# Linear attention and a Hyena gate on one core: two stretches of a hand-written order re-ordered, six output buffers, the last output tile in two halves

## The chip, the cores and the metric

The kernel runs on one core of a Trainium2 chip. The metric is the device time of one execution in microseconds (us). The engines are TensorE (PE, with its weight loads as PEld), VectorE (DVE), ScalarE (ACT), GpSimd (POOL) and SyncE (SP), which here only issues DMAs.

## The reference

Eight batches, eight heads, 576 positions, 64 features per head. First a linear attention per batch b and head h, then a gate with a long convolution over the 576 positions of each batch:

```python
def phi(x):                                   # w_phi: 64 x 128
    proj = x @ w_phi
    proj = proj - max(abs(proj), axis=-1)
    return concat([exp(proj), exp(-proj)])    # 256 features
q_p, k_p = phi(q), phi(k)
kv  = einsum('bhsf,bhsd->bhfd', k_p, v);  z = sum(k_p, over s)
x   = einsum('bhsf,bhfd->bhsd', q_p, kv) / (einsum('bhsf,bhf->bhs', q_p, z) + 1e-6)
x   = x, heads side by side                   # 8 x 576 x 512
x1, x2, x3 = split(x @ w_proj)                # w_proj: 512 x 1536
conv = irfft(rfft(x2, over 576) * rfft(filter_fft, over 576))
out  = (x1 * conv * x3) @ w_out               # 8 x 576 x 512, float32
```

## The kernel before

The whole program is one string, `PLAN`, of some 1540 words. A word is a method's name, its arguments and, after `@`, the first PSUM bank (0 to 7) of its result. `run` walks through the words under a manual schedule: each engine gets its instructions in the order of the words, and so does each DMA queue (SP issues stores and transposes, POOL the loads, ACT some stores at the end). There are no loops over batches: the words of up to three batches are interleaved, so that PE projects keys of one batch while it finishes another. The dependencies between engines become semaphores by themselves. So the order of the words is the one thing that says what stands ahead of what on an engine, and the bank number says which earlier reader a matmul has to wait for.

The words that the text speaks of, with batch b, head pair v, chunk c or m:

- `load,k|q|v,b`: POOL issues the load of one batch of k, q or v (L595). `trh,k|q,b,X`: SP issues the transpose of half a batch, kn to kT or qn to qT (L607).
- `Pk` (L635), `Qn` (L642), `Pq` (L669, L675): projections by w_phi on PE. `maxk`, `maxq` (L715): DVE takes the maxima from PSUM. `ex` (L697): ACT's exponentials. `mhi`, `mlo` (L739), `trm` and `trme`: the maxima, split in two bf16 parts (mh), are transposed on PE and copied to mT.
- `vs` (L757): POOL multiplies v by the keys' factor. `KV` (L772), `NE` (L786): PE's sums. `rc` (L800), `xn` (L805): DVE divides. `trx` (L824): SP issues the transpose of a quarter of xn to xT. `ptx` and `ptxe` do the same for one quarter by PE and a copy.
- `f1` (L853) and `f2` (L859): sums and differences of xn (SD, then xf), on POOL or DVE, ahead of the Fourier matmuls `Ft` (L868) and `Fs` (L875). `Fe` copies their result to XF, on ACT (L297) or DVE (L299). `X2` (L894), `Y1` (L904) and `m3` (L908): the projection in the frequency domain, the product with the filter and a sum.
- `X1`, `X3` (L916): projections x1 and x3 on PE, 8 matmuls of 256 columns each. `X1e` copies x1 to x1s. `tm` (L957) multiplies x1 by x3. `I` (L969), `Ie` (L987), `Ip`, `Im` (L990): the inverse transform. `ym` (L1004): the gate's product yT.
- `O` (L1015): one output tile of 128 positions by 512 columns, four matmuls of 512 columns. `Oe` copies it from PSUM to an `o` buffer, on ACT or DVE (L297, L299). `st` (L1024) stores 64 rows of it. Tile c = 4 holds the last positions of a pair of batches.

The buffers are rings: `RING` gives a name's count, and `turn_of` hands the next buffer of the ring to whoever asks first. A buffer is written again when its last reader has ended; for `o` that is a store that has landed.

Of the kernel before, what the change touches and what calls it, by code (L numbers as in the profile page):

```python
# [24 lines left out]
RING = {'Ekp': 4, 'Ekm': 4, 'Eqp': 3, 'Eqm': 3, 'vp': 3, 'vm': 3, 'r': 4, 'o': 4, 'kn': 2, 'qn': 2,  # L25
# [93 lines left out]
maxq,5,2@0 Pq,4,1@2 ex,q,m,4,0@4 trh,k,6,0 ex,q,p,4,0@4 ex,q,m,4,1@2 O,2,0@7 Oe,DVE,2,0@7
ex,q,p,4,1@2 X2,3,3@6 Y1,3,3@6 st,SP,2,0,1 KV,4,0@4 Pk,5,0@0 Pq,4,3@6 maxk,5,0@0 O,2,3@2  # L120
KVe,ACT,4,0@4 trxt,3 trh,q,5,0 ex,q,m,4,3@6 m3,POOL,3,1 NE,4,0@4 rc,4,0@4 ex,q,p,4,3@6 X3,3,2@3
st,SP,2,1,0 m3,POOL,3,0 xn,4,0@4 KV,4,1@6 Oe,DVE,2,3@2 load,q,6 ex,k,m,5,0@0 tm,3,2@3 ex,k,p,5,0@0
Pq,4,2@4 NE,4,1@0 rc,4,1@0 KVe,ACT,4,1@6 xn,4,1@0 f1,POOL,4,0,1 ex,q,p,4,2@4 NE,4,3@6 X2,3,4@3
rc,4,3@6 xn,4,3@6 ex,q,m,4,2@4 Y1,3,4@3 X1t,3@0 X1te,ACT,3@0 f1,POOL,4,0,0 NE,4,2@4 X3t,3@6 I,3,1@0
rc,4,2@4 f2,POOL,4,0,0 Pk,5,1@2 Ie,3,1@0 xn,4,2@4 tmt,3@6 trx,4,0 Pkt,5@6 Ip,3,1@0 Pqt,4@4 Im,3,1@0
maxkt,5@6 exqt,p,4@4 X3,3,1@0 exqt,m,4@4 f1,POOL,4,1,0 tm,3,1@0 st,SP,2,1,1 X1,3,3@1 exkt,p,5@6
exkt,m,5@6 maxk,5,1@2 I,3,0@4 Ie,3,0@4 ym,POOL,3,1 X1e,ACT,3,3@1 I,3,2@6 Ie,3,2@6 NEt,4@0 Im,3,0@4
Ip,3,0@4 ex,k,m,5,1@2 Im,3,2@6 rct,4@0 Ip,3,2@6 X3,3,3@5 ym,POOL,3,0 ex,k,p,5,1@2 xnt,4,1@0
f1,POOL,4,1,1 I,3,3@6 Ie,3,3@6 trx,4,3 em,m,5,0 trx,4,1 st,SP,2,2,0 xnt,4,0@0 tm,3,3@5 Pk,5,3@2
em,p,5,0 Qn,5,1@0 Ip,3,3@6 Qnt,5@4 trx,4,2 Im,3,3@6 maxq,5,1@0 X1,4,1@6 X3,4,1@7 maxqt,5@4  # L130
ex,k,m,5,3@2 trh,q,6,0 st,SP,2,3,0 ex,k,p,5,3@2 X1e,ACT,4,1@6 Pk,5,2@0 ex,k,p,5,2@0 f2,POOL,4,0,1
tm,4,1@7 ym,POOL,3,3 ex,k,m,5,2@0 Qn,5,0@4 maxq,5,0@4 maxk,5,2@0 ym,POOL,3,2 X1,4,0@6 vs,POOL,m,5,0
O,3,0@7 Oe,DVE,3,0@7 X1,4,2@4 mhi,5 trh,k,6,1 maxk,5,3@2 f2,POOL,4,1,1 X1e,ACT,4,0@6 X1,4,3@5
Ft,4,0,0@6 X1e,ACT,4,3@5 mlo,POOL,5 f2,POOL,4,1,0 Fs,4,1@0 X1e,ACT,4,2@4 trh,q,6,1 Fs,4,0@6 X3,4,2@5
Fe,ACT,4,1@0 yt,ACT,3 em,p,5,1 Fe,ACT,4,0@6 st,SP,3,0,1 trm,5@4 Ft,4,1,0@2 Fs,4,2@2 Fs,4,3@0
tm,4,2@5 Fe,DVE,4,3@0 st,SP,2,2,1 trme,ACT,5@4 Fe,ACT,4,2@2 Pq,5,1@6 Pq,5,0@4 Pk,6,0@2 maxk,6,0@2
O,3,2@0 Oe,DVE,3,2@0 st,SP,2,3,1 X2,4,1@1 ex,q,p,5,1@6 ex,q,m,5,1@6 trh,k,7,1 st,SP,2,0,0
vs,POOL,p,5,1 X2,4,2@6 vs,POOL,p,5,0 Y1,4,1@1 X2,4,3@7 ex,q,m,5,0@4 em,m,5,1 vs,POOL,m,5,1
ex,q,p,5,0@4 Xl,ACT,4 Y1,4,2@6 KV,5,0@4 KVe,DVE,5,0@4 Pqt,5@0 exqt,m,5@0 X2,4,0@6 Y1,4,3@7 NE,5,0@4
rc,5,0@4 xn,5,0@4 load,q,7 exqt,p,5@0 load,v,6 KV,5,1@0 Y1,4,0@6 ex,k,m,6,0@2 Pq,5,3@4 ex,k,p,6,0@2  # L140
KVe,ACT,5,1@0 ex,q,m,5,3@4 NE,5,1@2 rc,5,1@2 st,SP,3,2,1 xn,5,1@2 X2,4,4@0 Pk,6,2@6 ex,q,p,5,3@4
Y1,4,4@0 st,SP,3,0,0 m3,POOL,4,1 Pq,5,2@2 ex,q,m,5,2@2 ex,q,p,5,2@2 maxk,6,2@6 NE,5,3@4 rc,5,3@4
O,3,1@0 Oe,ACT,3,1@0 O,3,3@1 NE,5,2@2 m3,POOL,4,0 xn,5,3@4 O,3,4@0 Oe,DVE,3,3@1 ex,k,p,6,2@6
ex,k,m,6,2@6 rc,5,2@2 xn,5,2@2 NEt,5@4 rct,5@4 xnt,5,1@4 xnt,5,0@4 I,4,3@2 f1,POOL,5,0,1 X3,4,0@1
Ie,4,3@2 Ip,4,3@2 f1,DVE,5,1,1 f1,POOL,5,0,0 trxt,4 f2,DVE,5,0,0 tm,4,0@1 Oe,ACT,3,4@0 X1t,4@0
I,4,1@4 X1te,ACT,4@0 f1,DVE,5,1,0 Ie,4,1@4 Im,4,3@2 Ft,5,0,0@6 trx,5,3 st,SP,3,3,1 Ip,4,1@4
f2,POOL,5,0,1 X3t,4@2 Fs,5,1@0 trx,5,0 Fe,ACT,5,1@0 tmt,4@2 load,v,7 Fs,5,0@6 Im,4,1@4 f2,POOL,5,1,1
f2,POOL,5,1,0 X3,4,3@3 Fe,ACT,5,0@6 Ft,5,1,0@4 tm,4,3@3 Pk,6,1@6 trx,5,1 Fs,5,3@0 ym,POOL,4,1
# [52 lines left out]
class Kernel:  # L201
# [819 lines left out]
    def st(self, eng, b, c, i):  # L1021
        o = self.turn_of("o", (b, c))
# [58 lines left out]
```

## Time and profile before

| what | value |
|---|---|
| time of three runs | 299.99, 297.97, 295.18 us (median 297.97) |
| the profiled execution | 295.91 us, its span 294.0 us |
| busy | PE 272.7, DVE 248.8, ACT 223.5, POOL 229.4 us |
| mean granted clock of TensorE | 0.996 |
| DMA | 40.07 MB, mean 136 GB/s |

The profile shows one execution. "L916" is line 916 of the kernel; "a<-b" names a tile written and a tile read; "PEld" is the weight load, which overlaps with matmuls; "SPq" is SP's DMA queue, where the length of a row is how long SP needed to issue. A bracket at a row's end tells how long the engine was idle before it and what ended that.

### The profile page before, as it was taken

How to read it: one execution, taken by the hardware profiler on the slowest of the kernel's cores; microseconds unless marked ns; L12 is line 12 of the kernel's file. 1: busy time of each engine (PE TensorE's matmuls, PEld its weight loads, DVE VectorE, ACT ScalarE, POOL GpSimd, SP SyncE). 2: the span in 40 equal slices, each digit the busy share in tenths (PEclk: the TensorE clock that was granted, in tenths of full speed). 3: DMA queues.
4: the chain of work that ended last, by engine and by line, in shares of the span. 5: the costliest groups of instructions: out<-in, count | busy, mean ns of one | idle time of the engine just before them, and what ended most of it. 6: DMA issues, size and time to landing. Idle time of an engine off the chain costs nothing.

```text
span 294.0 us, 10233 instructions
## 1 busy us (share of the span) xinstructions
PE 272.7 (93%) x4297; PEld 194.9 (66%) x4332; DVE 248.8 (85%) x433; ACT 223.5 (76%) x371; POOL 229.4 (78%) x187
## 2 busy tenths in 40 slices
PE   5688999998999999999999999999999999999992
PEld 1346677666667856877478876776777666976750
DVE  6997899999989887999788978888999957687771
ACT  4999999987957787986897978968558999632421
POOL 8398894999867899999997899866948779855130
PEclk9999999999999999999999999999999999999998
DMA  7999999999899999999969945999282531222266
GB/s 138 240 207 163 164 197 168 123 203 181 131 157 199 151 162 195 161 107 187 172 112 138 211 95 108 161 138 180 61 98 50 90 75 28 21 45 56 61 130 188
DMA packets 72191, 40.07 MB, mean 136 GB/s; under 512 B 52496, under 2 KB 66960, under 8 KB 72144
## 3 DMA queue, kind: packets, MB, share of 16 engines
q1 hardware_dynamic: 56928, 22.49, 47.7%
q0 software_dynamic: 14816, 16.25, 36.7%
q8 instruction: 34, 0.56, 0.8%
q10 hardware_dynamic: 400, 0.66, 0.8%
q14 instruction: 13, 0.11, 0.1%
HBM read 33.75 MB, written 9.44 MB: 147 GB/s over the span
## 4 chain that ended last, share of the span: by engine, by line
PE 63%; DVE 5%; DMA 4%; issue 2%; ACT 2%; POOL 1%; SPq 0%; DVEq 0%; ACTq 0%; POOLq 0%
PE ps L916 15%; PE ps L894 10%; PE ps L1015 8%; PE ps L969 7%; PE ps L772 5%; PE ps L786 4%; PE ps L875 2%; PE ps L925 2%; PE ps L669 2%; PE ps L635 2%; DMA qT<-qn 2%; PE ps L675 2%; DVE mq L715 2%; PE ps L642 2%; DMA xT<-xn 1%
## 5 line engine op out<-in xcount | busy, mean ns | idle before, releaser
L916 PE MATMUL ps<-xT,wproj 128*128 128x256 bf16 x512 | 64.1, 273 | 0.5 <-DMA xT<-xn 0.4
L916 PEld LDWEIGHTS <-wproj 128*128 128x128 bf16 x512 | 48.1, 98 | 9.5 <-issue 0.6
L1004 POOL TENSOR_TENSOR yT<-cv,x1s 128x576 bf16<-128x576 f32 x31 | 39.3, 1278 | 18.5 <-DVE cv L990 16.9
L715 DVE TENSOR_REDUCE mq<-ps 128x8 f32<-128x1024 f32 (+1 forms) x40 | 43.7, 1110 | 4.1 <-PE ps L642 3.6
L715 DVE TENSOR_REDUCE mk<-ps 128x8 f32<-128x1024 f32 (+1 forms) x40 | 43.9, 1111 | 3.8 <-PE ps L635 2.6
L757 POOL TENSOR_TENSOR vm<-vn,vm 128x1152 bf16<-128x1152 bf16 x16 | 34.3, 2152 | 5.9 <-ACT vm L751 5.9
L757 POOL TENSOR_TENSOR vp<-vn,vp 128x1152 bf16<-128x1152 bf16 x16 | 34.4, 2155 | 5.6 <-ACT vp L751 5.5
L853 POOL TENSOR_TENSOR SD<-xn 128x512 bf16<-128x512 bf16 x28 | 32.0, 1153 | 7.0 <-DVE xn L805 5.4
L697 ACT ACTIVATE Eqp<-ps 128x1024 bf16<-128x1024 f32 x32 | 33.1, 1039 | 4.6 <-PE ps L675 4.5
L859 POOL TENSOR_TENSOR xf<-SD 128x512 bf16<-128x512 bf16 x27 | 30.8, 1155 | 6.7 <-DVE SD L853 6.2
L1015 PE MATMUL ps<-wout,yT 128*128 128x512 bf16 x127 | 34.8, 379 | 1.1
L697 ACT ACTIVATE Ekp<-ps 128x1024 bf16<-128x1024 f32 x32 | 33.1, 1034 | 1.9 <-PE ps L635 1.4
L697 ACT ACTIVATE Ekm<-ps 128x1024 bf16<-128x1024 f32 x32 | 33.1, 1033 | 1.3 <-DVE mk L715 0.9
L697 ACT ACTIVATE Eqm<-ps 128x1024 bf16<-128x1024 f32 x32 | 32.8, 1040 | 1.5 <-PE ps L675 1.1
L990 DVE TENSOR_TENSOR cv<-es,ps 128x288 f32<-128x288 f32 x64 | 26.4, 443 | 6.5 <-POOL yT L1004 3.7
L908 POOL TENSOR_TENSOR T<-T,T 128x1024 bf16<-128x1024 bf16 x14 | 29.6, 2127 | 2.7 <-DVE T L904 1.9
L894 PE MATMUL ps<-wproj,XF 128*128 128x512 bf16 x116 | 30.0, 379 | 1.2 <-ACT x1s L297 0.4
L969 PE MATMUL ps<-inv,T 128*128 128x288 bf16 x192 | 28.1, 286 | 0.7 <-DVE mq L715 0.4
L297 ACT COPY o<-ps 128x512 f32<-128x512 f32 x23 | 13.5, 596 | 15.9 <-PE ps L1015 13.7
L957 DVE TENSOR_TENSOR x1s<-ps,x1s 128x512 bf16<-128x512 f32 x32 | 21.8, 684 | 3.5 <-PE ps L916 2.2
L297 ACT CAST XF<-ps 128x576 bf16<-128x576 f32 x28 | 16.9, 647 | 9.2 <-PE ps L875 9.2
L297 ACT CAST x1s<-ps 128x512 bf16<-128x512 f32 (+1 forms) x32 | 16.9, 538 | 8.6 <-PE ps L916 4.2
(183 smaller groups left out, 638.2 us busy)
## 6 DMA issues: line engine op xcount, KB each, us to landing
out_dram<-o SPq DMA_DIRECT2D x67, 128.0 KB, 2.5
vn<-in_v_dram POOLq DMA_DIRECT2D x8, 576.0 KB, 8.4
kn<-in_k_dram POOLq DMA_DIRECT2D x7, 576.0 KB, 8.9
qn<-in_q_dram POOLq DMA_DIRECT2D x7, 576.0 KB, 7.9
wproj<-in_moe_w_proj_dram POOLq DMA_DIRECT2D x3, 512.0 KB, 7.8
fl<-in_moe_filter_fft_dram SPq DMA_DIRECT2D x8, 128.0 KB, 6.2
out_dram<-o ACTq DMA_DIRECT2D x5, 128.0 KB, 2.8
qn<-in_q_dram POOLq DMA_DIRECT2D x2, 288.0 KB, 7.1
```

The lines of the kernel that those rows point to most:

```text
L297: self.nc.scalar.copy(dst, src)
L697: self.nc.scalar.activation(e, p, AF.Exp, bias=0.0, scale=1.0 if g == "p" else -1.0)
L715: self.nc.vector.tensor_reduce(out=out, in_=src, axis=AX.X, op=ALU.max, apply_absolute_value=True)
L757: self.eng(eng).tensor_tensor(out=t[:, :, :, 0:64], in0=self.at("vn", b)[:, 2 * X:2 * X + 2], in1=t[:, :, :, 64:65].to_broadcast([128, 2, ...
L853: self.eng(eng).tensor_tensor(out=o[:, :, 2 * i:2 * i + 2, :], in0=x[:, :, 0:2, :], in1=x[:, :, 2:4, :], op=ALU.subtract if i else ALU.add)
L859: self.eng(eng).tensor_tensor(out=o[:, :, 2 * i:2 * i + 2, :], in0=x[:, :, 0:4:2, :], in1=x[:, :, 1:4:2, :], op=ALU.subtract if i else ALU ...
L894: self.mm(self.pb(0), l, w[:, kt, 512:1024], start=(kt == 0), stop=(kt == 3))
L908: self.eng(eng).tensor_tensor(out=Y, in0=Y, in1=self.at(f"T{2 * e + 1}", b), op=ALU.add)
L916: self.mm(o[:, d], w[:, kt, f0 + 128 * m:f0 + 128 * m + 128], y[:, 1, ::-1, ::-1] if d else y[:, 0], start=(kt == 0), stop=(kt == 3))
L969: self.mm(self.pb(e, 0, 288), l, inv[:, 2 * e + i if i < 2 else 4 + e, :], start=(i == 0), stop=(i == 2))
L1004: self.eng(eng).tensor_tensor(out=self.at("yT", b)[:, m, 0:SEQ], in0=self.turn_of("cv", (b, m)).rearrange("p x h t -> p (x h t)"), in1=sel ...
L1015: self.mm(self.pb(0), y[:, kt, 128 * c:128 * c + 128], w[:, kt, :], start=(kt == 0), stop=(kt == 3))
```

## The change

1. The stretch of the plan that runs at about 80 to 150 us (batches 1 to 3, called A below) is written in a new order with other PSUM banks. The stretch behind it keeps its order and gets other banks; the one word in it that moves is `load,v,5`, which stood ahead of the gate's products of batch 2 and now stands behind `f1,POOL,4,1,0`.
2. The stretch at about 195 to 262 us (batches 4 to 7, called B) is written in a new order, with other banks, and some words move up to the end.
3. In both, some words change engine. In A one output copy and one XF copy go from ACT to DVE. In B two output copies and two XF copies go from ACT to DVE, `f2,6,1,0` from POOL to DVE, one x1s copy and `trme,6` from DVE to ACT, `mlo,6` from DVE to POOL.
4. The ring `o` has six buffers for four.
5. The last output tile is computed, copied and stored in two halves of 256 columns (new words `Oh`, `Oeh`, `sth`), both stores on SP; before, one copy and two stores of 64 rows, on SP and ACT.

A cut of the diff: the ring, the piece of B around `X1,6,0`, the end of the plan, the new functions.

```diff
-RING = {'Ekp': 4, ... 'r': 4, 'o': 4, 'kn': 2, 'qn': 2,
+RING = {'Ekp': 4, ... 'r': 4, 'o': 6, 'kn': 2, 'qn': 2,
...
-mlo,POOL,7 f1,POOL,6,1,0 trx,6,2 O,5,3@5 f2,POOL,6,0,1 exkt,p,7@0 ptx,6,3@4 ptxe,DVE,6,3@4
-f2,POOL,6,1,0 f2,POOL,6,1,1 Oe,ACT,5,3@5 O,5,1@6 exkt,m,7@0 Oe,DVE,5,1@6 O,5,0@4 maxk,7,2@2 X1,6,0@7
-Pk,7,1@0 Oe,ACT,5,0@4 maxk,7,1@0 Ft,6,0,5@2 em,m,7,1 Fs,6,1@5 trm,7@4 em,p,7,1 X1e,ACT,6,0@7
-Fs,6,0@2 Fe,ACT,6,1@5 Fe,ACT,6,0@2 trme,DVE,7@4 em,p,7,0 ex,k,m,7,1@0 X1,6,1@7 Ft,6,1,4@2 Fs,6,2@2
...
+ex,k,p,7,2@4 f1,POOL,6,1,0 Oe,DVE,5,3@1 f1,POOL,6,1,1 exkt,p,7@2 f2,POOL,6,1,1 O,5,1@1 exkt,m,7@2
+trx,6,2 trme,DVE,7@6 Oe,ACT,5,0@7 Pk,7,1@2 maxk,7,2@4 Ft,6,0,6@4 Fs,6,0@4 Fs,6,1@6 em,m,7,1
+Oe,DVE,5,1@1 ptxe,DVE,6,3@0 ex,k,m,7,1@2 Fe,ACT,6,0@4 X1,6,0@1 maxk,7,1@2 Fe,ACT,6,1@6 X1,6,1@0
+f2,DVE,6,1,0 X1e,ACT,6,0@1 Ft,6,1,6@4 Fs,6,2@4 Fs,6,3@6 Fe,DVE,6,2@4 ex,k,p,7,1@2 X1,6,2@1
...
-st,SP,7,3,0 O,7,1@7 yt,DVE,7 Oe,ACT,7,1@7 st,SP,7,0,1 O,7,2@6 st,ACT,7,1,1 Oe,DVE,7,2@6 st,ACT,7,2,0
-st,SP,7,1,0 O,7,4@7 st,SP,7,2,1 st,ACT,7,0,0 Oe,DVE,7,4@7 st,SP,7,4,1 st,ACT,7,4,0
+yt,DVE,7 Oe,ACT,7,1@3 st,SP,7,0,1 O,7,2@2 st,ACT,7,1,1 Oe,DVE,7,2@2 st,ACT,7,2,0 st,SP,7,1,0
+Oh,7,4,0@5 Oh,7,4,1@7 st,SP,7,2,1 st,ACT,7,0,0 Oeh,DVE,7,4,0@5 sth,SP,7,4,0 Oeh,DVE,7,4,1@7
+sth,SP,7,4,1
...
+    def Oh(self, b, c, h):
+        y, w, x = self.at("yT", b - (c == 4)), self.at("wout"), slice(256 * h, 256 * h + 256)
+        for kt in range(4):
+            self.mm(self.pb(0, 0, 256), y[:, kt, 128 * c:128 * c + 128], w[:, kt, x],
+                    start=(kt == 0), stop=(kt == 3))
+    def Oeh(self, eng, b, c, h):
+        self.copy(eng, self.turn_of("o", (b, c))[:, 256 * h:256 * h + 256], self.pb(0, 0, 256))
+    def sth(self, eng, b, c, h):
+        o, x = self.turn_of("o", (b, c)), slice(256 * h, 256 * h + 256)
+        dict(SP=self.nc.sync, ACT=self.nc.scalar)[eng].dma_start(
+            out=self.out.rearrange("b (t j) d -> (b t) j d", j=9)[64 * b - 64:64 * b + 64, 4, x],
+            in_=o[:, x])
```

The functions behind `Oeh` move down by 15 lines and those ahead of them by one, so a line of the page stands one or 16 lower in the changed kernel.

How the order moves on SP in stretch A, near 125 to 142 us of the profile before. kT1 and qT1 are the transposed keys and queries of batch 5, xT1 that of batch 3, o0 to o5 the output buffers. Before:

```order
L824 DMA_TRANSPOSE xT1_134<-xn0_130 128x4x128 x4
L607 DMA_TRANSPOSE kT1_85<-kn1_79 128x9x128
L1024 DMA out_0_dram<-o0_1174 64x512
L1024 DMA out_0_dram<-o1_1175 64x512
L607 DMA_TRANSPOSE kT1_85<-kn1_79 128x9x128
L1024 DMA out_0_dram<-o0_1174 64x512
L1024 DMA out_0_dram<-o3_1177 64x512
L607 DMA_TRANSPOSE qT1_83<-qn1_77 128x9x128
L1024 DMA out_0_dram<-o2_1176 64x512
L607 DMA_TRANSPOSE kT0_84<-kn0_78 128x9x128
```

And now, on the same queue:

```order
L608 DMA_TRANSPOSE kT1_85<-kn1_79 128x9x128
L1040 DMA out_0_dram<-o4_1178 64x512
L825 DMA_TRANSPOSE xT1_134<-xn0_130 128x4x128 x4
L608 DMA_TRANSPOSE kT1_85<-kn1_79 128x9x128
L608 DMA_TRANSPOSE qT1_83<-qn1_77 128x9x128
L1040 DMA out_0_dram<-o5_1179 64x512
L1040 DMA out_0_dram<-o2_1176 64x512
L1040 DMA out_0_dram<-o1_1175 64x512
L1040 DMA out_0_dram<-o0_1174 64x512 x2
L1040 DMA out_0_dram<-o5_1179 64x512
L608 DMA_TRANSPOSE kT0_84<-kn0_78 128x9x128
```

The first kT1 goes ahead of the four xT1 transposes, and qT1 follows the second kT1 with no store between; six stores stand behind it.

On DVE in stretch B, near 226 to 243 us of the profile before, from the maxima of batch 7's keys (mk1) to the first product of Y1 (T20). Before:

```order
L715 TENSOR_REDUCE mk1_87<-ps_61 128x2x4
L715 TENSOR_REDUCE mk1_87<-ps_61 128x2x2
L299 COPY xT0_133<-ps_61 128x512
L299 COPY o0_1174<-ps_61 128x512
L715 TENSOR_REDUCE mk1_87<-ps_61 128x2x4 x2
L299 COPY mT1_93<-ps_61 128x128
L299 CAST x1s0_141<-ps_61 128x2x8x32 x2
L904 TENSOR_TENSOR T20_1165<-ps_61,HTo0_71 128x1024
```

And now:

```order
L716 TENSOR_REDUCE mk1_87<-ps_61 128x2x4
L716 TENSOR_REDUCE mk1_87<-ps_61 128x2x2
L300 COPY o5_1179<-ps_61 128x512
L300 COPY mT1_93<-ps_61 128x128
L716 TENSOR_REDUCE mk1_87<-ps_61 128x2x4
L300 COPY o1_1175<-ps_61 128x512
L300 COPY xT0_133<-ps_61 128x512
L716 TENSOR_REDUCE mk1_87<-ps_61 128x2x4
L860 TENSOR_TENSOR xf0_138<-SD0_137 128x2x256
L300 CAST XF0_139<-ps_61 128x576 x2
L300 CAST x1s0_141<-ps_61 128x2x8x32 x2
L905 TENSOR_TENSOR T20_1165<-ps_61,HTo0_71 128x1024
```

One more output copy, an f2 (xf0) and two XF copies stand ahead of the x1s copies, and the two maxima are parted by an output copy and the xT copy.

On DVE at the end, from the last gate product. Before:

```order
L957 TENSOR_TENSOR x1s0_141<-ps_61,x1s0_141 128x2x8x32
L1004 TENSOR_TENSOR yT1_1173<-cv1_1171,x1s0_141 128x576
L299 COPY o3_1177<-ps_61 128x512
L299 COPY yT0_1172<-yT1_1173 128x4x64
L299 COPY o2_1176<-ps_61 128x512
L299 COPY o3_1177<-ps_61 128x512
```

And now:

```order
L958 TENSOR_TENSOR x1s0_141<-ps_61,x1s0_141 128x2x8x32
L1005 TENSOR_TENSOR yT1_1173<-cv1_1171,x1s0_141 128x576
L300 COPY o1_1175<-ps_61 128x512
L300 COPY yT0_1172<-yT1_1173 128x4x64
L300 COPY o4_1178<-ps_61 128x512
L300 COPY o5_1179<-ps_61 128x256 x2
```

The last copy no longer writes the buffer that the first of these rows' copies used, and it is two copies of 256 columns.

More of the change, by code (lines that the diff above doesn't have):

```diff
@@ L119 @@
[L119 to L124, printed above, removed]
@@ L137 @@
[L137 to L142, printed above, removed]
@@ L143 @@
[L143 to L148, printed above, removed]
```

212 lines of the change are left out of this document (115 added, 97 removed).

## The prediction

> **What bounds the kernel now.** I read the page first: busy shares, the chain that ended last, the costliest group.
>
> ```profile
> PE 272.7 (93%) x4297; PEld 194.9 (66%) x4332; DVE 248.8 (85%) x433; ACT 223.5 (76%) x371; POOL 229.4 (78%) x187
> ...
> PE 63%; DVE 5%; DMA 4%; issue 2%; ACT 2%; POOL 1%; SPq 0%; DVEq 0%; ACTq 0%; POOLq 0%
> ...
> L916 PE MATMUL ps<-xT,wproj 128*128 128x256 bf16 x512 | 64.1, 273 | 0.5 <-DMA xT<-xn 0.4
> ```
>
> PE is busy for 93% of the span and carries 63% of the chain. So a new order, which removes no matmul, can give back only what PE idles inside the two stretches. The windows measure that; their columns are the window, its length, then busy time and instructions of PE, weight loads, DVE, ACT and POOL, and at the end the granted clock, the DMA share and GB/s.
>
> ```profile
> 80.00:150.00 70.00, 68.16 (x1021) 48.97 (x1029) 61.35 (x92) 54.45 (x95) 62.44 (x48) 1.00 1.17 167
> 195.00:262.00 67.00, 64.82 (x1057) 47.76 (x1061) 56.78 (x94) 49.14 (x84) 50.76 (x35) 1.00 0.46 77
> 220.00:230.00 10.00, 9.43 (x227) 7.78 (x226) 9.39 (x17) 8.88 (x13) 7.09 (x6) 1.00 0.20 43
> 230.00:240.00 10.00, 8.90 (x108) 5.68 (x107) 8.47 (x15) 9.46 (x17) 8.95 (x9) 1.00 0.55 87
> ```
>
> The first stretch (80 to 150 us, A) leaves PE idle for 70.00 - 68.16 = 1.84 us, the second (195 to 262 us, B) for 67.00 - 64.82 = 2.18 us, of which 0.57 + 1.10 = 1.67 us lie between 220 and 240 us. The clock is 1.00 in all four, so nothing is to be had there. The waits of PE name who ends them: the first two rows are of A, the last of B (us in total, times, longest).
>
> ```profile
> PE ps L642 <- DMA qT<-qn: 0.7, 1, 0.7
> PE ps L635 <- DVE mq L715: 0.4, 1, 0.4
> ...
> PE ps L916 <- DMA xT<-xn: 0.4, 1, 0.4
> ```
>
> In each stretch one late transfer stands first; the rest are waits for a PSUM bank that DVE's maxima or ACT still read, none above 0.4 us. They are shown somewhat short: a 256-column matmul is listed with 273 ns, but six follow each other in 0.82 us (the chain, below), 137 ns each, so a modelled end can hide about 0.14 us of a real wait.
>
> **Stretch A.** The wait of 0.7 us is for the qT transpose of the first half of batch 5's queries. SP's own timeline shows why it is late.
>
> ```profile
> 131.05 3.00 SPq L607 DMA_TRANSPOSE kT<-kn  x1
> 134.14 1.18 SPq L1024 DMA_DIRECT2D out_dram<-o  x2
> 135.38 1.45 SPq L607 DMA_TRANSPOSE kT<-kn  x1
> 136.87 1.24 SPq L1024 DMA_DIRECT2D out_dram<-o  x2
> 138.22 1.31 SPq L607 DMA_TRANSPOSE qT<-qn  x1
> ...
> 143.26 0.40 PE L642 MATMUL ps<-wphi,qT 64*128 64x128 bf16 x8 [0.66 <-DMA qT<-qn]
> ...
> DMA to landing us min/median/max: 3.3/4.8/6.5
> ```
>
> The transpose issues at 138.22 and lands at the 143.2 that PE waits for, 5 us on, near the 4.8 of the last row (landing times of qT). After the change it follows the second kT transpose directly, and four stores go behind it: 1.18 + 1.24 = 2.42 us earlier on SP. A wait of 0.66 shown, with 0.14 hidden, is less than 2.42, so it goes: **-0.8 us**. The words ahead of the matmul on PE are the same in kind, so nothing else pulls it forward by that much. The four stores come later by one issue of 1.3 us each; six buffers instead of four let the evictions go on meanwhile. Without them that delay would come back to ACT, whose 54.45 of 70 us hide it.
>
> The other 1.84 - 0.66 = 1.18 us of A are bank and maximum waits below 0.4 us each. The new order changes the neighbours of nearly all; a bank wait removed in one place can reappear in the next. Bounds 0 and -1.2; I take **-0.5**.
>
> What A adds: one output copy goes from ACT to DVE and one more XF copy to DVE. The rows by form price them.
>
> ```profile
> L299 DVE COPY o<-ps 128x512 f32<-128x512 f32 x13 | 8.9, 687 | 3.7 <-PE ps L1015 3.1 <-DMA out_dram<-o 0.4
> L299 DVE CAST x1s<-ps 128x512 bf16<-128x512 f32 x8 | 5.4, 683 | 1.7 <-PE ps L916 1.3 <-ACT XF L297 0.4
> L299 DVE CAST XF<-ps 128x576 bf16<-128x576 f32 x4 | 3.0, 755 | 3.0 <-PE ps L875 3.0
> L859 DVE TENSOR_TENSOR xf<-SD 128x512 bf16<-128x512 bf16 x5 | 1.9, 417 | 0.0
> ```
>
> That is 0.687 + 0.755 = 1.44 us for DVE, beside 70.00 - 61.35 = 8.65 us in which it is idle.
>
> **The load of v for batch 5** moves down POOL's queue, to behind the f1 that started at 161.55 us before the change, where POOL has hardly a gap.
>
> ```profile
> L595 POOL DMA_DIRECT2D vn<-in_v_dram x8: 750/792/812, 6.5 to 192.1; - x8
> ...
> 161.55 1.16 POOL L853 TENSOR_TENSOR SD<-xn 128x512 bf16<-128x512 bf16 x1
> 162.94 1.28 POOL L1004 TENSOR_TENSOR yT<-cv,x1s 128x576 bf16<-128x576 f32 x1 [0.23 <-DVE x1s L957]
> ...
> 170.74 2.15 POOL L757 TENSOR_TENSOR vm<-vn,vm 128x1152 bf16<-128x1152 bf16 x1
> ...
> 174.16 1.16 POOL L859 TENSOR_TENSOR xf<-SD 128x512 bf16<-128x512 bf16 x1
> ...
> 175.74 0.49 PEld L875 LDWEIGHTS <-xf 128*128 128x128 bf16 x8 [0.24 <-issue]
> ...
> vn<-in_v_dram POOLq DMA_DIRECT2D x8, 576.0 KB, 8.4
> ```
>
> POOL pays 0.79 us for it. Queued behind are ym products (L1004, the first at 162.94), f1 and f2 pieces, and the product with v (L757) at 170.74; then f2 of batch 4 ends at 174.16 + 1.16 = 175.32 and PE loads it at 175.74. Slack 0.4 against 0.8 of delay: **+0.35 us**. The transfer itself issues by about 162.9 and lands 8.4 us later at 171.3; the product, 0.8 late, would start at 171.5, just after. At worst it lands some 2 us later and PE then waits 2.6; at best the gaps swallow all (0).
>
> **Stretch B.** The chain around 230 us, in order of time:
>
> ```profile
> 228.04 0.69 DVE xn L805
> ...
> 231.78 0.61 DVE xn L805
> ...
> 233.28 4.04 DMA xT<-xn
> ...
> 237.37 0.82 PE ps L916 x6
> 238.18 0.33 PE ps L635 x8
> 238.51 0.25 PE ps L868 x4
> 238.76 0.37 PE ps L875 x4
> ```
>
> The third xT transpose of batch 6 is in flight for 4.04 us, and the x1 projection (L916) that needs it begins at 237.37, when it lands; a k projection (0.33), Ft (0.25) and Fs (0.37) stand behind it. In the new order k projection, Ft and both first Fs stand ahead of it: 0.95 us and more of work under the transfer, against a wait of 0.4 shown: **-0.5** with what is hidden. The rest of B's idle time, 2.18 - 0.4 = 1.8 us, is bank waits beside DVE's maxima, which keep their order between 223 and 230 us, where DVE is busy for 9.39 of 10 us. A third of it: **-0.6**, bounds 0 and -1.8.
>
> What B adds to DVE: two output copies (+1.374), two XF copies (+1.51) and one f2 (+0.417) come, one x1s copy (-0.683) goes; a copy of mT and a difference of mh go too, which I don't credit. +2.6 us beside 67.00 - 56.78 = 10.2 us idle. Of A's and B's 4.1 us I expose **+0.5**, one part in eight, as nearly all idle time of DVE in these rows lies beside PE's work; the bounds are 0 and 4.1.
>
> **The tail.** ACT's copy of the first tile of batch 7 waits for an o buffer, DVE's last copy likewise.
>
> ```profile
> 286.57 1.07 ACT L297 COPY o<-ps 128x512 f32<-128x512 f32 x2 [2.08 <-DMA out_dram<-o]
> ...
> 288.95 0.69 DVE L299 COPY o<-ps 128x512 f32<-128x512 f32 x1 [0.41 <-DMA out_dram<-o]
> ...
> L990 DVE TENSOR_TENSOR cv<-es,ps 128x288 f32<-128x288 f32 x64 | 26.4, 443 | 6.5 <-POOL yT L1004 3.7 <-ACT es L987 2.7 <-PE ps L650 0.2
> L299 DVE COPY yT<-yT 128x256 bf16<-128x256 bf16 x1 | 0.2, 217 | 0.0
> ```
>
> Six buffers end both waits, but PE's last matmuls end no earlier, since they queue for PE itself. The halves cost PE eight matmuls of 256 columns for four of 512, the same columns. The first half is copied while PE works on the second, so after PE's end one copy of 256 columns is left in the place of one of 512. The trace has no such copy from PSUM; the nearest rows are 443 ns (288 columns from PSUM, with a second operand) and 217 ns (256, bf16, no PSUM). I take 0.44, nearest in kind: 0.69 - 0.44 = 0.25, and 0.05 of the buffer wait: **-0.3**. With the low price and the whole buffer wait it is -0.9; if the two copies run one behind the other after PE's end, 0.88 - 0.69 = +0.2. Both stores now stand on SP, but the first is issued during the second copy.
>
> The Trainium skill, "VectorE: DVE Perf Modes", section "The TRN2 errata — SBUF-src ops pay a fixed extra latency per instruction", speaks against the split: a copy from PSUM costs 120 cycles plus one per column at 0.96 GHz, and it advises tiles of at least 512. By that estimate 512 columns take 0.66 us, which agrees roughly with the row's 0.687, and two halves 0.78; the tail term would be +0.1 with both copies behind PE and -0.27 with one, before the buffer wait.
>
> **Sum** against the profiled execution, 295.91 us (span 294.0): -0.8 - 0.5 - 0.5 - 0.6 - 0.3 + 0.35 + 0.5 = -1.85, so 294.1. The three timed runs have their median at 297.97 and spread from 295.18 to 299.99; the mean of these and the profiled one is 297.3, the base I use for the change's time: **295.4**.
>
> **Rivals.** (1) The waits only move: a new order keeps the sum of small waits, and only the qT wait and the tail are gained, with the costs in full: -0.8 - 0.3 + 0.85 = -0.25, 297.0. For it: no single wait besides qT's passes 0.4. (2) Slower: DVE becomes the bound. Its extra copies stand ahead of the maxima that free PE's banks; from the point where a 10 us piece leaves DVE less idle time than it is given (0.61 us in 220 to 230), each extra us is PE's. With all 4.1 exposed, less 0.3 for the tail, +3.8: 301.1. Against it: 8.65 and 10.2 us of idle time. (3) The new order really fits: both stretches lose all idle time shown, 4.0 us, with the tail's 0.3 and 0.14 hidden in each of five waits: -5.0, 292.3. Against it: the chain of maxima is unchanged. (4) f2 of batch 6 now runs on DVE beside POOL's sister f2, both reading bf16 from SBUF.
>
> ```profile
> L859 POOL TENSOR_TENSOR xf<-SD 128x512 bf16<-128x512 bf16 x27 | 30.8, 1155 | 6.7 <-DVE SD L853 6.2
> ```
>
> If the two exclude each other, DVE stands for one POOL f2, 1.15 us, in the busy piece of B: 296.5. The Trainium skill, "SBUF — State Buffer", section "SBUF: two separate sides", says just this: the two engines share a port pair under an exclusive lock, taken by a DVE operation with two SBUF inputs, and the other blocks until it ends. No run here shows it.
>
> **How the numbers follow.** Forecast 295.4: 0.40; (1) 0.22; (2) 0.12; (3) 0.16; (4) 0.10. The range, 291.2 to 299.6, takes in all but (2) and the fast end of (3), with some 1 to 2 us for the spread of executions. Two per cent, about what a measurement of this kernel can tell, is 292.0 and 303.9: faster 0.13 (under half of (3) and a tail of the forecast), slower 0.04 (a third of (2)), the same 0.83.
>
> **What would show it.** In the changed profile: no wait of L643 on qT near 143 us; PE busy within 1.3 us of the whole in A and 1.2 in B; no o wait of ACT in the tail and two half copies near 0.44; f2 of batch 4 ending 0.8 later and PE waiting for it. Wrong, if PE's waits on maxima grow to 1 us or more in either stretch, if the product with v waits for its load, or if the time leaves 294 to 297 without one of these.

## The result and the profile after

The changed kernel takes 293.67 us in the median of 22 runs (292.74 to 297.52), the kernel before 295.89 us in 22 runs taken beside them (294.51 to 299.99). The ratio is 0.9928, with a 95% interval of 0.9908 to 0.9947: 2.2 us or 0.7% faster, well under 2%. Runs more than 1.5% above the fastest of their kernel are left out of the ratios and of the medians in the experiments. The profiled execution after took 293.02 us with a span of 291.2, so 2.9 us and 2.8 us less than the profiled one before.

The page after, its busy row and its chain:

```profile
PE 274.0 (94%) x4336; PEld 194.8 (67%) x4336; DVE 252.3 (87%) x438; ACT 221.9 (76%) x367; POOL 228.5 (78%) x187
...
PE 71%; DVE 3%; ACT 2%; issue 1%; DVEq 0%; ACTq 0%
```

DVE is busy for 3.5 us more, as the added copies would have it. The chain that ended last is 71% PE, and DMA, 4% of it before, is no longer in it. The same windows as before:

```profile
80.00:150.00 70.00, 70.00 (x1112) 50.37 (x1111) 64.33 (x95) 55.93 (x94) 63.31 (x47) 1.00 1.08 160
195.00:262.00 67.00, 66.06 (x1072) 48.41 (x1070) 58.95 (x95) 49.35 (x84) 51.64 (x37) 1.00 0.42 77
...
220.00:230.00 10.00, 9.19 (x238) 7.79 (x236) 9.60 (x19) 8.75 (x13) 8.35 (x8) 1.00 0.24 50
230.00:240.00 10.00, 9.87 (x103) 6.11 (x100) 8.80 (x15) 8.76 (x16) 6.86 (x7) 1.00 0.46 72
```

PE shows no idle time in A (1.84 us before) and 0.94 in B (2.18). The piece from 230 to 240 us went from 1.10 idle to 0.13; the one from 220 to 230 us went the other way, 0.57 to 0.81, because other work stands in it now. Of PE's waits for a transfer or for DVE's maxima none is listed any more between 80 and 262 us; one for ACT's exponentials is left:

```profile
PE ps L787 <- ACT Eqm L698: 0.3, 1, 0.3
```

Where the time went is read from four pieces of PE work that both plans have in the same role: KV of batches 2, 4 and 6 (first row of each) and the last sixteen matmuls of X1 and X3. The first column is the start. Before, then after:

```profile
88.61 0.43 PE L772 MATMUL ps<-vp,Ekp 64*128 64x65 bf16 x16
...
150.25 0.43 PE L772 MATMUL ps<-vp,Ekp 64*128 64x65 bf16 x16
...
211.70 0.42 PE L772 MATMUL ps<-vp,Ekp 64*128 64x65 bf16 x16
...
281.10 1.91 PE L916 MATMUL ps<-xT,wproj 128*128 128x256 bf16 x16
```

```profile
88.91 0.43 PE L773 MATMUL ps<-vp,Ekp 64*128 64x65 bf16 x16
...
148.70 0.43 PE L773 MATMUL ps<-vp,Ekp 64*128 64x65 bf16 x16
...
210.00 0.42 PE L773 MATMUL ps<-vp,Ekp 64*128 64x65 bf16 x16
...
278.23 1.91 PE L917 MATMUL ps<-xT,wproj 128*128 128x256 bf16 x16
```

The execution after is 0.30 us late at 88 us, in work that the change doesn't touch, 1.55 early at 149, 1.70 early at 210 and 2.87 early at 278. So A gave 1.85 us, the middle 0.15, and B 1.17. From the last mark to the end of the span it took 12.90 us before and 12.97 after: the tail gave nothing.

SP's queue in A, and the tail:

```profile
132.00 1.38 SPq L608 DMA_TRANSPOSE kT<-kn  x1
133.48 1.31 SPq L608 DMA_TRANSPOSE qT<-qn  x1
134.89 3.75 SPq L1040 DMA_DIRECT2D out_dram<-o  x6
```

```profile
283.80 1.07 ACT L298 COPY o<-ps 128x512 f32<-128x512 f32 x2 [2.17 <-PE ps L1016]
...
284.93 1.37 DVE L300 COPY o<-ps 128x512 f32<-128x512 f32 x3 [1.76 <-PE ps L1016]
286.44 1.12 SPq L1033 DMA_DIRECT2D out_dram<-o  x2
```

qT issues 4.7 us sooner than the 138.22 of before. In the tail ACT's copies of batch 7 wait for PE and no longer for a buffer, and the last row of copies holds the whole copy of tile 2 and the two halves without a gap. (The profile puts an earlier copy, at 281.04 us, down to a landing, but it starts 2.81 us after the last mark, as in the kernel before.) The prediction named these signs; its other sign, PE waiting for f2 of batch 4, isn't there.

### The profile page after: what moved, and what is told of

It is laid out like the page before. It is cut to its first block, busy times and chain, and to the rows that moved or that the text cites. A ratio compares the mean times of both kernels' runs of the same rounds, so it can differ in the third digit from the quotient of the medians.

```text
span 291.2 us, 10275 instructions
## 1 busy us (share of the span) xinstructions
PE 274.0 (94%) x4336; PEld 194.8 (67%) x4336; DVE 252.3 (87%) x438; ACT 221.9 (76%) x367; POOL 228.5 (78%) x187
## 4 chain that ended last, share of the span: by engine, by line
PE 71%; DVE 3%; ACT 2%; issue 1%; DVEq 0%; ACTq 0%
PE ps L917 17%; PE ps L895 11%; PE ps L1016 10%; PE ps L970 8%; PE ps L773 5%; PE ps L787 4%; PE ps L876 3%; PE ps L926 2%; PE ps L670 2%; PE ps L636 2%; PE ps L643 2%; PE ps L676 2%; PE ps L869 2%; DVE mq L716 1%; PE ps L796 1%
## 5 line engine op out<-in xcount | busy, mean ns | idle before, releaser
L860 POOL TENSOR_TENSOR xf<-SD 128x512 bf16<-128x512 bf16 x26 | 29.7, 1155 | 6.4 <-DVE SD L854 5.9
L895 PE MATMUL ps<-wproj,XF 128*128 128x512 bf16 x128 | 31.6, 379 | 0.3 <-ACT x1s L298 0.3
L298 ACT COPY o<-ps 128x512 f32<-128x512 f32 x20 | 11.8, 600 | 14.4 <-PE ps L1016 12.0
L806 DVE TENSOR_TENSOR xn<-ps,r 128x512 bf16<-128x512 f32 x32 | 21.9, 689 | 0.9
```

Source lines behind the costliest of these rows:

```text
L298: self.nc.scalar.copy(dst, src)
L860: self.eng(eng).tensor_tensor(out=o[:, :, 2 * i:2 * i + 2, :], in0=x[:, :, 0:4:2, :], in1=x[:, :, 1:4:2, :], op=ALU.subtract if i else ALU ...
L895: self.mm(self.pb(0), l, w[:, kt, 512:1024], start=(kt == 0), stop=(kt == 3))
```

## The experiments

Each was compared with the kernel before on the same chip. To tell what a kernel changes from what an execution changes, I took the starts of the same PE work in every profile. The table gives, for each kernel, how much earlier (-) or later (+) PE came, against the first profile before, across five pieces of the program; the last column is the time from the last X1/X3 mark to the end of the span, good to 0.05 us, as spans are listed to 0.1.

| kernel | A, 95 to 114 us | at Qn behind qT, 143 us | batch 4's X1, 160 to 181 us | 186 us | B, 191 to 271 us | tail |
|---|---|---|---|---|---|---|
| before | 0 | 0 | 0 | 0 | 0 | 12.90 |
| before_again | 0.0 | -0.1 | 0.0 | -0.2 | +0.1 | 12.99 |
| o6_only | 0.0 | -0.7 | 0.0 | -0.2 | -0.2 | 13.26 |
| tail_only | 0.0 | -0.7 | 0.0 | -0.2 | -0.6 | 13.47 |
| b_only | 0.0 | -0.7 | 0.0 | -0.2 | -1.2 | 12.93 |
| a_only | -1.0 | -0.7 | +0.1 | -0.2 | +1.1 | 12.84 |
| a_fix | -1.0 | -0.7 | +0.6 | -0.2 | -0.2 | 12.80 |
| the change | -1.0 | -0.7 | +0.1 | -0.2 | -1.2 | 12.97 |
| after_o4 | -1.0 | -0.7 | +1.2 | -0.2 | -1.1 | 13.33 |
| after_whole | -1.0 | -0.7 | +0.1 | -0.2 | -1.2 | 12.85 |
| after_tail2 | -1.0 | -0.7 | +0.5 | -0.2 | -1.2 | 13.04 |
| load_back | -1.0 | -0.7 | 0.0 | -0.2 | -1.2 | 13.22 |
| load_back_whole | -1.0 | -0.7 | 0.0 | -0.2 | -1.2 | 12.91 |

Two columns are steady: the new order of A gives 1.0 us between 95 and 114 us, the new order of B 1.2 us, in every profile of the table that has them. The old order of B itself lies between +0.1 and -0.6, as its wait for xT near 237 us differs, so against another profile of the old order B's gain would be 0.6 to 1.3 us. The +1.1 of a_only is a slip told below; dve_back, which changes both stretches, stands with its own experiment. The column at 186 us is the first profile's own: its wait is not even in the second profile of the same kernel. 0.4 us of the tails of o6_only and tail_only are a wait of PE for DVE's x1s that no other profile lists.

**The kernel before, profiled again** (no edit).

> The kernel before, profiled once more. Theory 1 (its waits of 0.7 us for qT near 143 us and 0.6 us for xT near 237 us are landings that differ from one execution to the next, and its waits behind DVE's maxima near 102 to 106 and 224 to 232 us do not): the second group is there again within 0.1 us, the first is shorter or gone. Rival (all waits belong to the order): both groups again as in the first profile.

```profile
PE ps L635 <- DVE mq L715: 0.6, 2, 0.4
PE ps L642 <- DMA qT<-qn: 0.6, 1, 0.6
PE ps L916 <- DMA xT<-xn: 0.5, 1, 0.5
```

295.55 us. The waits behind the maxima are there again, as expected; but so are those for qT and xT, within 0.1 us. For this kernel the rival is right: all but the wait at 186 us come back.

**Six buffers alone.**

```diff
-'r': 4, 'o': 4,
+'r': 4, 'o': 6,
```

> The kernel before with six output buffers for four and nothing else. Theory 1: ACT's and DVE's waits for an output buffer in the tail are gone from the profile, PE's end does not move, and the last copy starts at most 0.1 us earlier: 0 to -0.1 us. Rival: the buffers alone are worth the tail's 0.3 us.

295.80 us in the median, ratio 1.0021 (1.0005 to 1.0037): no gain, rather 0.2% lost. In its profile the buffer waits of the tail are gone and the last copy waits for PE instead:

```profile
288.00 0.69 DVE L299 COPY o<-ps 128x512 f32<-128x512 f32 x1 [0.30 <-PE ps L1015]
```

Unexpectedly, the wait for qT at 143 us is gone too, with SP's order untouched. The issue of qT is 1.0 us sooner (0.3 to 1.0 in the three profiles with six buffers and the old order of A, counted from the mark at 88 us), and what changes most is the time to landing (queue view of 132 to 145 us, before and six buffers; the last column is us to landing):

```profile
qT<-qn SPq DMA_TRANSPOSE x1, 5.0
```

```profile
qT<-qn SPq DMA_TRANSPOSE x1, 3.5
```

It is 5.0 and 4.9 us in the two profiles with four buffers, and 3.5, 3.3 and 3.4 in the three that have six and the old order of A. The traces show what parts them. For half a microsecond or more near 142 us the DMAs move next to nothing in all five profiles: 14 GB/s from 142.5 to 143.0 us in the kernel before, where it was 167 to 231 from 140.5 to 142.0. With six buffers qT lands ahead of that stretch, at 140.67, 141.10 and 141.61 us, with four behind it, at 143.21 and 143.09. What stops the DMAs there, I did not find out. PE's end in the tail was expected not to move, and it came 0.4 us later after the mark, by the wait for x1s. The profiled execution, 295.01 us, is also the fastest of this kernel's twelve, so its waits may be below the usual; the median, which moved the other way, is not explained.

**The tail alone** (six buffers and the two halves, orders as before).

```diff
-O,7,4@7 st,SP,7,2,1 st,ACT,7,0,0 Oe,DVE,7,4@7 st,SP,7,4,1 st,ACT,7,4,0
+Oh,7,4,0@4 Oh,7,4,1@7 st,SP,7,2,1 st,ACT,7,0,0 Oeh,DVE,7,4,0@4 sth,SP,7,4,0 Oeh,DVE,7,4,1@7 sth,SP,7,4,1
```

> The kernel before with six output buffers and the last tile in two halves, orders of A and B as before. Theory 1 (SP's queue takes the gain: the last two stores and the one ahead of them issue one behind the other): the last copy ends 0.4 to 0.5 us earlier after PE's O of tile 2, the last store still issues at the same time within 0.2 us, and the time is the same within 0.2 us. Rival (the prediction's term): the time is 0.3 us (0.1%) shorter, and the last store issues 0.3 us earlier.

295.85 us, ratio 1.0017 (0.9998 to 1.0037), the same as with six buffers alone. From O of tile 2 on, the last copy ended after 2.65 us, with six buffers alone after 2.96, while the last store issued at 3.52, there at 3.24, since SP holds both halves behind a store of tile 2. That is the expected direction, against the predicted 0.3 us, though the copy gained less than the expected 0.4 to 0.5 and the store came more than 0.2 later.

**Stretch B alone** (new order of B, six buffers, old order of A, whole last tile; the bank numbers of B renumbered so that they meet the old ones of the middle).

```diff
-... the words from number 1060 on in the old order
+... the same words in the new order, banks 6, 5, 4, 0, 2, 7, 3, 1 back to 2, 7, 6, 4, 0, 3, 1, 5
```

> The new order of stretch B, six output buffers, and the old order of stretch A and an undivided last tile. Theory 1: PE's work on the last tile comes 1.1 to 1.2 us (0.4%) earlier against the start of B, most of it between 220 and 240 us, with waits of PE on DVE's maxima left near 225 to 232 us. Rival: DVE, given 2.2 us more here, is late for stretch B when A has not given it time, and less than 0.5 us is gained.

294.56 us, ratio 0.9966 (0.9932 to 1.0000), 0.9 us below the 295.44 of the runs beside it. Windows of 212 to 242 us, before and with B alone:

```profile
212.00:242.00 30.00, 28.17 (x493) 20.90 (x488) 26.03 (x43) 24.96 (x44) 21.72 (x17) 1.00 0.52 81
```

```profile
212.00:242.00 30.00, 28.96 (x485) 21.33 (x480) 28.37 (x48) 24.43 (x41) 20.56 (x18) 1.00 0.30 57
```

PE works 0.8 us more in the same 30 us, with DVE at 28.37 of 30.00. Its marks moved by 1.2 us, theory 1's number; DVE is fuller than before and is not late by it.

**Stretch A alone, with a slip.** The new order of A with the moved load and six buffers; the old B renumbered into the new banks.

```diff
-... the words from 437 on to 1060 in the old order
+... the same words in the new order; from 1060 on the old order, banks 2, 7, 6, 4, 0, 3, 1, 5 as 6, 5, 4, 0, 2, 7, 3, 1
```

> The new order of stretch A with the moved load of v, six output buffers, and the old order of stretch B and the old tail. Theory 1 (each stretch gives back the waits it held by itself): the first matmul of KV for batch 4 comes 1.8 us earlier against the start of stretch A than in the kernel before, of which 0.8 at the Qn that waits for qT, and the time is 1.8 us (0.6%) shorter. Rival 1 (the prediction's terms as sized): 1.3 us at that place, 0.35 given back at the moved load, so 0.9 us (0.3%). Rival 2 (a gain in A is eaten in B, since B's waits are on DVE and transfers that keep their own pace): at most 0.3 us left at the end.

296.26 us, ratio 1.0035 (1.0002 to 1.0069): nothing gained. KV of batch 4 does come 1.85 us earlier against the mark at 88 us, the place and size of theory 1, but B then gives 1.1 back. (The profiled execution, 294.89 us, is 1.0 below that of the kernel before; that the median isn't is as unexplained as with six buffers alone.) The profile has a wait that no other has:

```profile
PE ps L868 <- DVE mk L715: 1.1, 1, 1.1
```

Ft of batch 6 uses a pair of banks, 5 and 6 before. The renumbering sends 5 to 1 and 6 to 4, but a pair must be neighbours, so Ft used 1 and 2, and 2 is the bank of the maxima just ahead. This was my edit's doing. The second form gives Ft the pair 4 and 5 and the transposed maxima bank 6 (in old numbers), before renumbering:

```diff
-Ft,6,0,5@2 ... Fs,6,1@5 ... trm,7@4 ... Fe,ACT,6,1@5 ... trme,DVE,7@4
+Ft,6,0,4@2 ... Fs,6,1@4 ... trm,7@6 ... Fe,ACT,6,1@4 ... trme,DVE,7@6
```

> As a_only, but Ft, Fs and Fe of batch 6 use another pair of PSUM banks: in a_only the renumbered banks let Ft,6,0 share a bank with the maxima of batch 7's keys, and PE waited 1.3 us for it there. Theory 1 (that wait was made by my bank numbers; stretch A gives back its waits on maxima): no such wait; PE comes 1.0 us earlier at KV,3,1, keeps that to O,7,2 against the kernel with six buffers alone, and the time is 0.9 to 1.1 us (0.3%) below that kernel's 295.8, so 294.8. Rival (B eats what A gains): the time stays within 0.3 us of 295.8.

294.64 us, expected 294.8; ratio 0.9975 (0.9944 to 1.0005). The wait is gone and A keeps its 1.0 us. The two ratios, 0.9975 and 0.9966, multiply to 0.9941, where the whole change has 0.9928: the stretches add up within the intervals.

**The change with four buffers.**

```diff
-'r': 4, 'o': 6,
+'r': 4, 'o': 4,
```

> The changed kernel with four output buffers. Theory 1 (the new order puts six stores behind the transposes, so evictions need the two more buffers): ACT or DVE wait for an output buffer at 140 to 150 us and PE's banks behind them, 0.5 to 2 us longer than the changed kernel. Rival 1: the buffers matter in the tail only, where ACT's wait for one returns: 0 to 0.3 us. Rival 2 (six buffers alone measured 0.2% above the kernel before, so they cost something): 0.3 to 0.6 us shorter.

294.46 us, ratio 0.9949 (0.9909 to 0.9988), 0.8 us above the change's 293.67, with overlapping intervals. No engine waits for an output buffer near 145 us. In the tail the waits are back (ACT 2.1 us, DVE 0.5): the last copy ends 0.6 us later after the mark than in the change, and the tail takes 13.33 us for 12.97, the place and about the size that rival 1 gave. The profile's larger loss is elsewhere:

```profile
PE ps L917 <- DMA xT<-xn: 1.2, 1, 1.2
```

X1 of batch 4 waits 1.2 us for its transposed input, a wait that the kernel before doesn't have there. It is in the profiles of a_fix (0.6 us) and after_tail2 (0.4 us) too, both with six buffers. So it doesn't come from the buffers; what those kernels share is the moved load. In a_fix and after_o4 the product with v also waits 0.4 us for that load.

**The change with the load of v back.**

```diff
-trh,q,5,1 ... f1,POOL,4,1,0 tm,3,1@2 st,SP,2,1,1 X1,3,3@3 exkt,p,5@4 load,v,5 exkt,m,5@4
+trh,q,5,1 load,v,5 ... f1,POOL,4,1,0 tm,3,1@2 st,SP,2,1,1 X1,3,3@3 exkt,p,5@4 exkt,m,5@4
```

> The changed kernel with the load of v for batch 5 back at its old place, 20 us earlier. Theory 1 (where the change put it, the load's 576 KB share the DMA engines with the xT transposes of batch 4 and the qT and kT transposes behind them, and X1 of batch 4 then waits for xT: 0, 0, 0.4, 0.6 and 1.2 us in five profiles with the moved load): no wait of L917 for xT between 165 and 180 us, the transposes issue there in 1.3 to 2 us each, not 2.3 to 3, and the time is 0.3 to 0.6 us shorter on the mean. Rival 1 (the xT wait comes from PE being 1 us earlier in the new order, not from the load): the wait stays. Rival 2 (the prediction: POOL's 0.79 us is what the move costs): f2 of batch 4 ends 0.8 earlier, 0.35 us shorter, with the transposes as long as before.

The queue view of 156 to 168 us, after_o4 (the load at 161 us), then with the load back:

```profile
vn<-in_v_dram POOLq DMA_DIRECT2D x1, 576.0 KB, 8.4
xT<-xn SPq DMA_TRANSPOSE x3, 7.2
qT<-qn SPq DMA_TRANSPOSE x1, 7.2
kT<-kn SPq DMA_TRANSPOSE x1, 6.4
```

```profile
qn<-in_q_dram POOLq DMA_DIRECT2D x1, 576.0 KB, 6.1
xT<-xn SPq DMA_TRANSPOSE x4, 5.5
qT<-qn SPq DMA_TRANSPOSE x2, 3.4
kT<-kn SPq DMA_TRANSPOSE x1, 3.5
```

With the load beside them the transposes of q and k land in 6.4 to 7.5 us in the change, after_whole, after_tail2, a_fix and after_o4 (in a_only too); without, in 3.4 to 3.8 by these views, in the kernel before as well. X1's wait is 0, 0, 0.4, 0.6 and 1.2 us in those five, and none in the two profiles with the load back. For the landings that is theory 1; for the wait it fits, but two of the five have none either. The 0.3 to 0.6 us that theory 1 expected are not there: 293.54 us, ratio 0.9934 (0.9903 to 0.9964), for 0.9928 of the change. Its profiled execution came 1.6 us late to 88 us, in untouched work, which is the size of all that is looked for here.

**The tail's stores on both queues.**

```diff
-st,ACT,7,2,0 st,SP,7,1,0 Oh.. st,SP,7,2,1 st,ACT,7,0,0 Oeh,DVE,7,4,0@5 sth,SP,7,4,0
+st,ACT,7,0,0 st,ACT,7,2,0 st,SP,7,1,0 Oh.. st,SP,7,2,1 Oeh,DVE,7,4,0@5 sth,ACT,7,4,0
```

> The changed kernel with its last stores spread over both queues: the first half's store on ACT in the place of SP, and ACT's store of tile 0 ahead of that of tile 2. Theory 1 (SP's queue holds the last store): SP issues the second half's store when its copy ends, the last issue is 0.6 to 0.7 us earlier after O,7,2 (from 3.5 to 2.8 us), and the span is 0.4 to 0.7 us shorter from O,7,2 on. Rival (landing, not issue, sets the end: the last stores share the DMA engines): the last issue moves, the end of the span less than 0.2 us.

294.34 us, ratio 0.9957 (0.9917 to 0.9997). Its last stores and the last copies:

```profile
285.36 1.37 DVE L300 COPY o<-ps 128x512 f32<-128x512 f32 x3 [1.76 <-PE ps L1016]
286.87 0.69 SPq L1033 DMA_DIRECT2D out_dram<-o  x1
287.24 0.55 ACTq L1033 DMA_DIRECT2D out_dram<-o  x1
```

The last issue came 0.35 us sooner after PE's mark (287.24 - 278.66 = 8.58 us; in the change the second of SP's two starts at 287.16 - 278.23 = 8.93), and yet the span ended 13.04 us after the mark, for 12.97. The traces tell when the stores land: the last one 11.80 us after the mark here and 11.79 in the change, and in all fourteen profiles the span ends 1.2 us after it. So the rival is right: at the end of this kernel it is the landing of the last stores, not when they issue, that sets the time. My theory that SP's queue took the gain finds no support; as the same stores leave tails of 12.97 and 13.22 us in the change and in load_back, one profile can't exclude a part of it.

**The change with an undivided last tile.**

```diff
-Oh,7,4,0@5 Oh,7,4,1@7 st,SP,7,2,1 st,ACT,7,0,0 Oeh,DVE,7,4,0@5 sth,SP,7,4,0 Oeh,DVE,7,4,1@7 sth,SP,7,4,1
+O,7,4@3 st,SP,7,2,1 st,ACT,7,0,0 Oe,DVE,7,4@3 st,SP,7,4,1 st,ACT,7,4,0
```

> The changed kernel with an undivided last tile: one copy, two stores of 64 rows on SP and ACT. Theory 1 (the halves' gain at the copy is used up in SP's queue): the last copy ends 0.4 us later after O,7,2 than in the changed kernel, the last stores land within 0.15 us of it, and the time is the same within 0.2 us. Rival (the prediction's term): 0.3 us longer.

293.62 us, ratio 0.9925 (0.9900 to 0.9951): the same as the change. The last copy ends 0.37 us later (3.02 for 2.65 us after O of tile 2), and the tail takes 12.85 us for 12.97. The halves bring nothing; in the three pairs of profiles that differ by them alone they cost 0.1 to 0.3 us (12.97 for 12.85, 13.47 for 13.26, 13.22 for 12.91).

**DVE's new copies back on ACT.**

```diff
-Oe,DVE,1,3  Fe,DVE,2,2  Oe,DVE,4,3  Oe,DVE,5,3  Fe,DVE,6,2  Fe,DVE,6,3
+Oe,ACT,1,3  Fe,ACT,2,2  Oe,ACT,4,3  Oe,ACT,5,3  Fe,ACT,6,2  Fe,ACT,6,3
```

> The changed kernel with six of the copies that it gave to DVE back on ACT at the same places (three o copies, one XF copy in A, two in B): 4.3 us less for DVE, 3.7 more for ACT. Theory 1 (DVE's extra copies stand in idle time and cost PE nothing): the time is the same within 0.4 us. Rival 1 (the prediction's term, 0.5 us exposed): 0.5 us shorter. Rival 2 (ACT is the tighter one there, since its exponentials free the banks of the maxima): 0.5 to 2 us longer, with waits of PE on ACT in 224 to 242 us.

299.49 us, ratio 1.0118 (1.0085 to 1.0151): 5.8 us above the change, 3.8 above the kernel before. Rival 2 in direction, and by more than it said; its place, 224 to 242 us, holds only a part. Of the waits of PE these are new:

```profile
PE ps L773 <- issue: 1.3, 1, 1.3
PE ps L895 <- ACT XF L298: 1.0, 1, 1.0
...
PE ps L670 <- ACT XF L298: 0.5, 1, 0.5
PE ps L917 <- ACT o L298: 0.5, 1, 0.5
```

Read from the same marks, A gives 0.4 us up to 114 us for 1.0, then loses 2.6 between 115 and 124, where the change gains or loses nothing, and B loses 1.0 where the change gains 1.2. Not all of it is ACT's: X1 of batch 4 waits 0.8 us for xT, the wait that goes with the moved load, and what ends the longest new wait (1.3, "issue") the profile doesn't show. In the new order ACT has no room for these copies, though in the change it is busy for 56 of 70 us in A and DVE for 64. The share of busy time pointed the wrong way.

**The two hints together**: the load back and the last tile undivided.

> The changed kernel with the load of v back and an undivided last tile: the version that the runs so far point to. Theory 1: as load_back, and the span from O,7,2 on is 0.1 us shorter (7.48 for 7.59): 0.4 to 0.7 us below the changed kernel's 293.67, so 293.1, and no xT wait near 170 us in this second profile either. Rival: the load collides at 141 us with the stores and transposes there, and PE waits for qT or kT between 140 and 150 us for 0.5 us or more: no gain.

292.79 us in the median (292.49 to 294.11), ratio 0.9902 (0.9868 to 0.9936). It is the fastest of all, 0.9 us below the change's median (0.7 by what each gains on the kernel before beside it), though the intervals overlap. Its profile has no wait for xT near 170 us, none for qT or kT near 145 us, and a tail of 12.91 us.

## Why the prediction was right, and where not

The forecast was -1.9 us to 295.4; measured are -2.2 us in the medians and 293.67 us. Sign and size hold. By its own last sign the prediction failed all the same: the time left 294 to 297 without one of its other signs of being wrong. The time itself lies 1.7 us below because of the base: the three runs known then, with a median of 297.97, stood high in what became 22 runs with a median of 295.89. The mean of 297.3 that I chose was too high by 1.4; the profiled execution's 295.91 was the better base. The size is in part luck: with what is measured below (-0.7, -1.0, -1.2, 0.4 on the mean for the load, nothing for DVE and the tail) the terms add up to -2.5, and a gain in A sized 0.5 too small and a cost of DVE 0.5 too large are offset in part by the tail's 0.3. Of the rivals, (1) is refuted in A, where the small waits went and didn't move; (3) came in A, and in B for over half of the idle time. Term by term:

- **qT, -0.8**: -0.72 in the profile, at the place named. But the reason is shared: six buffers alone remove the same wait in three profiles of three, by an earlier landing. The prediction had given the buffers no part in it. An earlier transpose with four buffers in the old order was not run.
- **The rest of A, -0.5**: mis-sized; it is -1.0 in all eight profiles with the new order of A in the table. I took half of 1.18 us of shown idle time. Of this, 0.6 us were gaps of missing matmul records (last section) and 0.54 stand at 102 to 105 us: in the kernel before, the two Pk of batch 3 there,

```profile
102.69 0.63 PE L635 MATMUL ps<-wphi,kT 64*128 64x128 bf16 x8
...
105.03 0.40 PE L635 MATMUL ps<-wphi,kT 64*128 64x128 bf16 x8 [0.39 <-DVE mq L715]
```

and in the changed kernel:

```profile
102.81 0.39 PE L636 MATMUL ps<-wphi,kT 64*128 64x128 bf16 x8
...
104.11 0.40 PE L636 MATMUL ps<-wphi,kT 64*128 64x128 bf16 x8
```

The second no longer waits for DVE's maxima, the first no longer takes 0.24 us longer than its like, and the Qnt ahead of it starts 0.2 us sooner behind its predecessor; the profile names a releaser for the 0.39 alone. A modelled matmul end hides part of each wait, which I credited to the transfers and not to these.
- **B, -0.5 and -0.6**: -1.1 to -1.2 in all seven profiles with its new order. The split cannot be told: the first wait differs between profiles (0.5, 0.4, 0.2, 0.2 and none in five with the old order of B), and the marks between 230 and 270 us belong to moved words.
- **The load, +0.35**: the wrong mechanism. POOL's 0.79 us cost PE nothing; f2 never was late, since the issue fell where POOL had idled 0.23 and 0.58 us ahead of its two ym products: the prediction's best case. A cost came through the transfers: the transposes beside the load take twice the time to land, and in those profiles PE waits 0 to 1.2 us for xT, 0.4 on the mean of five. The range given to it (0 to 2.6) holds; the row to look at was the queue at the new place, not POOL's.
- **DVE's copies, +0.5**: no cost found. The same copies on ACT cost 5.8 us with the rest unchanged, so in this order the swap is what makes room. Rival 2, DVE as the bound, did not come: in the window where DVE is busy for 9.60 of 10 us the profile lists no wait of PE for DVE.
- **The tail, -0.3**: nothing, 12.97 for 12.90 us, and 0.1 to 0.3 lost against the undivided tile. The price of a half copy (0.44) was right:

```profile
L300 DVE COPY o<-ps 128x256 f32<-128x256 f32 x2 | 0.8, 420 | 0.0
```

The step that failed is the one from the last copy to the end: I took the end as following the last copy by a fixed time. The end follows the last landing by a fixed 1.2 us, and a last copy 0.37 us sooner, or a last store 0.35 us sooner, left that landing where it was or made it later. Whether the last stores share a rate of the DMA engines or a fixed cost that smaller rows make longer was not separated.
- **The price of the split on DVE**: two half copies take 0.84 us for 0.687 of a whole one. The Trainium skill, "VectorE: DVE Perf Modes", section "The TRN2 errata — SBUF-src ops pay a fixed extra latency per instruction", gives 0.39 us a half as an estimate by its formula and advises tiles of 512 or more; the measured 0.420 is 7% above that. What the halves lose at the end doesn't come by that path, since DVE is done 4.9 us before the end of the span.
- **The shared port (rival 4)** was not put to the test. DVE's f2 of batch 6 took its usual 0.42 us, at a time when POOL ran nothing.

## What to carry to other kernels

When PE is the bound and a fixed order feeds it, count its waits one by one, from start to start, and ask of each whether it belongs to the order or to a transfer: the first kind came back in every profile, the second differed by up to 1.2 us between profiles with the same words there. A moved load is priced by what else is in the DMA queues where it lands, and a copy, as dve_back suggests, by what waits behind it on its engine, not by the engine's share of busy time. At the end of a kernel look at what lands last: work ahead of the last stores' landing gave nothing here.

## What the runs showed of the hardware that I had not expected

- A 576 KB load issued by POOL beside SP's transposes made them land in 6.4 to 7.5 us in six profiles, where the medians without it were 3.4 to 3.8 us. In a seventh, dve_back, they took 4.8 to 5.4.
- Two more buffers for output tiles, with SP's order as before, go with a qT transpose that lands in 3.3 to 3.5 us for 4.9 to 5.0 us: ahead of half a microsecond or more in which the DMAs nearly stand still, and not behind it. What stops them is open.
- Profiles differ by up to 1.7 us before the first 90 us are over, in work that no edit touched: the marks at 88 us lie between 88.6 and 90.3 us. A change of a few tenths can be read from marks within one profile, but not from a single time.
- The page before lists 4297 matmuls for 4332 weight loads, the page after 4336 for 4336. Each missing 512-column record leaves a gap that looks like 0.05 us of idle time in a window. A has nine such gaps and a tenth of 0.16 us, which other profiles don't have, so some 0.6 of the 1.84 us that I started from were no idle time at all.
